# Attention and soft mixture of experts in one kernel: V's rows through two buffers up to pair 9, and another order of the last two pairs

## The chip, the cores and the metric

One core of a Trainium2 chip runs the whole kernel as one program. The metric is the device time of one execution in microseconds, and three executions give a median. Its engines are TensorE (PE, with its weight loads as PEld), VectorE (DVE), ScalarE (ACT), GpSimd (POOL) and SyncE (SP), which only issues transfers here. Each engine runs its instructions in the order in which they were issued to it, and waits for others by semaphores.

## The reference

```python
def _attn_ref(q, k, v, n_global, n_local):      # q, k, v: (4, 8, 768, 64)
    scores = scale * np.matmul(q, k.transpose(0, 1, 3, 2))
    ...
    keep = is_global | is_local                 # 8 global keys, 96 local ones, causal
    ...
    scores = np.where(keep, scores + bias, -1e9)
    a = softmax(scores)
    return np.matmul(a, v)

def _moe_ref(x, phi, w1, w2):                   # x: (3072, 512), 32 slots, 8 experts
    logits = x @ phi
    d = softmax(logits, over tokens)
    slot_input = d.T @ x
    for e in range(8):
        slot_out[e] = np.maximum(slot_input[e] @ w1[e], 0) @ w2[e]
    c = softmax(logits, over slots)
    return c @ slot_out
```

The bias is a slope per head times the distance. The output of the attention, (4, 768, 8 x 64), is the x of the expert layer. Softmax stands for the reference's own lines, with its small term in the divisor.

## The kernel before

There are 16 pairs (u = 0 to 15): four batches of four pairs of heads. For each pair the attention runs these steps, with i the head of the pair, k a third of the scores and z a third of the probabilities:

- load_qk, load_v (L418, L422): the transfers of q and k, and of V's rows (448 KB), issued by SP.
- v_hi or v_hi_act (L521, L524): V scaled to float16, on POOL for odd pairs and on ScalarE for even ones, into one of two buffers. v_lo (L527): what float16 leaves over, on VectorE. It reads V's rows once more and is their last reader.
- scores (L533) on TensorE; biased (L547) on VectorE adds the bias table and takes the running maximum.
- max_t, max_r, max_b, max_c: the maximum over the pair, by TensorE, VectorE, TensorE and ScalarE in turn. exponential (L570): on ScalarE, per head, with that maximum.
- w_hi (L579, ScalarE) or w_hi_dve (L583, VectorE): the float16 high part of the probabilities of one head. w_lo (L587, POOL) or w_lo_dve (L591, VectorE): the low part of a third z of one head, 128 x 432 elements. Both engines run it at line 589. There is one buffer for high parts and one for low parts, so w_hi of the next pair's head waits until TensorE has read the old one.
- values (L594): on TensorE, 39 small matmuls per head, thirteen each of high by high, high by low and low by high.
- ev_sum, ev_rec, ev_mul: VectorE divides by the row sums and writes x. tr, tr_copy: transposed x by TensorE and ScalarE. logits, logits_half, logits_all: x @ phi, two pairs at a time. by_token, dispatch, dispatch_sum and others: the expert layer's dispatch, once in a batch.

All these steps stand in one hand-written list, ORDER (L56), which interleaves pairs: while values of pair u runs, scores of pair u + 2 or so are made. Each engine's own order follows from that list.

V's rows have one buffer, vraw (L358). A step ('load_v', u) issues the transfer once v_lo of pair u - 1 has read the buffer, and from pair 3 on it also issues a piece of the expert weights. The expert weights come in 32 pieces of 1 MB: steps 'piece' load twelve of them into buffers of their own (weights, 12 times 2048 columns of float32), and steps 'free' load others into the attention's buffers as they come free. All of them stand in SP's one queue with the loads of q, k and V, in ORDER's sequence.

After the list, last_dispatch finishes the dispatch, and then hidden, project and combine compute the experts and write the output from the same core.

Of the kernel before, what the change touches and what calls it, by code (L numbers as in the profile page):

```python
# [15 lines left out]
AF = mybir.ActivationFunctionType  # L16
ALU = mybir.AluOpType
# [4 lines left out]
B, H, S, D = 4, 8, 768, 64  # L22
# [4 lines left out]
NJ = 7  # L27
# [22 lines left out]
VC = NJ * 2 * D  # L50
TABW = 4 * QW
NW = 12
# [4 lines left out]
NP = H // 2  # L57
SW = 2 * KB
NEG = -1.0e30
V_SC = 2.0 ** 6  # L60
# [235 lines left out]
def tile_attention_moe(ctx: ExitStack, tc: tile.TileContext, qk, v, phi, w1, w2, nn, out):  # L296
    nc = tc.nc
# [29 lines left out]
    weights = [keep.tile([P, WP], F32, name=f"wp{i}") for i in range(NW)]  # L327
# [18 lines left out]
    xn01 = ap.tile([P, 2 * XH], F32, name="xn01")  # L346

    def own(name, w):

        return home_of[name] if name in home_of else ap.tile([P, w], F32, name=name)  # L350

    rq = [own(f"raw{i}", QKW) for i in range(2)]
    tbs = [own(f"tb{i}", TBW) for i in range(NTB)]
    whi = [own(f"hi{i}", HPW).bitcast(F16) for i in range(NHB)]
    wlo = [own(f"lo{i}", HPW).bitcast(F16) for i in range(NHB)]
    tabs = [own(f"tab{p}", TABW).bitcast(BF16).rearrange("p (i c) -> p i c", i=2) for p in range(NP)]
    by_head = "p (j i d) -> p j i d"
    vraw = own("vraw", VC).rearrange(by_head, j=NJ, i=2)  # L358
    v16 = [own(f"v{i}", VW) for i in range(2)]
    vhi = [w[:, 0:VHW].bitcast(F16).rearrange(by_head, j=NJ, i=2) for w in v16]  # L360
    vlo = [w[:, VHW:].bitcast(F16).rearrange(by_head, j=NJ, i=2) for w in v16]
    xn2 = own("xn2", XH)
    xnb = [a[0:KB].rearrange("p (t f) -> p t f", t=NJ) for a in (xn01[:, 0:XH], xn01[:, XH:], xn2)]
    xtb = [own(f"xt{i}", S) for i in range(3)]


    last = nu - 1
    spaces = []
    for name in leaves:
        t, a, b = used[name]  # L370
        spaces.append([(k, max(a, at) - at, min(b, at + WP) - at) for k, (bt, at) in enumerate(blocks) if bt is t and max(a, at) < min(b, at + WP)])
    held = []
    for name, i, *_ in ORDER:
        if name == "free":
# [25 lines left out]
    def load_w(pieces, c0=0, c1=WP):  # L400

        for k in pieces:
            m, e, half = piece(k)
            nc.sync.dma_start(out=places[k][:, c0:c1], in_=(w1, w2)[m][e][:, WP * half + c0:WP * half + c1])
# [17 lines left out]
    def load_v(u):  # L422
        nc.sync.dma_start(out=vraw, in_=v[u // NP, u % NP])
        if u > 2 and extras:
            k, c0, c1 = extras.pop(0)
            load_w([k], c0, c1)
# [51 lines left out]
    def late_constants():  # L478
        nc.gpsimd.tensor_tensor(out=i4, in0=ident[:, 0:32], in1=ident[:, 32:64], op=ALU.add)
        nc.gpsimd.tensor_tensor(out=i4, in0=i4, in1=ident[:, 64:96], op=ALU.add)  # L480
        nc.gpsimd.tensor_tensor(out=i4, in0=i4, in1=ident[:, 96:128], op=ALU.add)
        nc.gpsimd.memset(sl, 0.0)
# [38 lines left out]
    def v_hi(u):  # L521
        nc.gpsimd.tensor_scalar(out=vhi[u % 2][:, :, :, 0:D], in0=vraw, scalar1=V_SC, scalar2=0.0, op0=ALU.mult, op1=ALU.add)  # L522

    def v_hi_act(u):  # L524
        nc.scalar.activation(out=vhi[u % 2][:, :, :, 0:D], in_=vraw, func=AF.Copy, scale=V_SC)  # L525

    def v_lo(u):  # L527
        k = u % 2
        flat = "p j i d -> p (j i) d"
        nc.vector.scalar_tensor_tensor(out=vlo[k].rearrange(flat), in0=vraw.rearrange(flat), scalar=V_SC,  # L530
                                       in1=vhi[k].rearrange(flat)[:, :, 0:D], op0=ALU.mult, op1=ALU.subtract)
# [306 lines left out]
    def table_pair_act(p):  # L838
        table.pair(p, True)

    steps = dict(piece=piece_of, free=free, load_qk0=load_qk0, load_phis=load_phis, keys=keys, warm=warm,
                 table_even=table_even, table_odd=table_odd, table_pair=table_pair, table_pair_act=table_pair_act, load_qk=load_qk, load_v=load_v, v_hi=v_hi, v_hi_act=v_hi_act, v_lo=v_lo,
                 scores=scores, biased=biased, max_t=max_t, max_r=max_r, max_b=max_b, max_c=max_c, exponential=exponential, w_hi=w_hi, w_hi_dve=w_hi_dve, w_lo=w_lo, w_lo_dve=w_lo_dve,
                 values=values, ev_sum=ev_sum, ev_rec=ev_rec, ev_mul=ev_mul, tr=tr, tr_copy=tr_copy, tr_copy_dve=tr_copy_dve,
                 logits=logits, logits2=logits2, logits_half=logits_half, logits_all=logits_all, strip_max=strip_max, strip_exp=strip_exp,
                 strip_sum=strip_sum, by_token=by_token, by_token_copy=by_token_copy, lnat_copy=lnat_copy, dispatch=dispatch, dispatch_sum=dispatch_sum)
    late_constants()
    for name, u, *args in ORDER:
        steps[name](u, *args)
# [311 lines left out]
```

## Time and profile before

| what | value |
|---|---|
| median of three runs | 213.93 us (212.89, 213.93, 214.44) |
| the profiled execution | 211.82 us, of which 210.0 us are the span of its instructions |
| mean granted TensorE clock | 0.975 |
| TensorE, VectorE, ScalarE, POOL busy | 86%, 71%, 61%, 56% of the span |
| attention and dispatch | up to about 155 us |
| hidden, project and combine | about 155 to 198 us, the last transfers after that |
| DMA | 61.41 MB, 292 GB/s on average |

Times on the trace are counted from the start of the span. A row of the timeline reads: start, length (of all instructions that it merges), engine, line, operation, output<-input, shape, count, and in brackets how long the engine stood idle before it and what ended that. "wa" is the large block that holds most of the attention's buffers, "wp" an expert weight buffer, "x" and "m" are TensorE's output banks. The slices of the page are 5.25 us each.

### The profile page before, as it was taken

What the parts mean: (1) busy time and instruction counts of PE and PEld (TensorE: products, weight loads), DVE (VectorE), ACT (ScalarE), POOL (GpSimd) and SP (SyncE); (2) the same over time, 40 slices, a digit from 0 to 9 for tenths busy, and PEclk for the clock granted to TensorE, in tenths of its full rate; (3) what the DMA queues carried; (4) which work ended last, traced back from release to release, by engine and by line L of the source; (5) the groups of instructions that cost most, each with busy time, mean ns of one, the idle gap of its engine ahead of it and who ended that gap; (6) DMA issues with size and microseconds to landing.
All of it is one profiled execution on the core that took longest, in us unless ns stands there. A gap on an engine that the chain in (4) does not pass through costs nothing. (4 is left out here: it accounts for less than half of the span.)

```text
span 210.0 us, 6480 instructions
## 1 busy us (share of the span) xinstructions
PE 180.3 (86%) x2649; PEld 128.2 (61%) x2649; DVE 150.1 (71%) x376; ACT 127.7 (61%) x177; POOL 117.9 (56%) x142
## 2 busy tenths in 40 slices
PE   8779899879599989999999999787799999998300
PEld 2356688658387868878788886565343266655200
DVE  3989999499788878988888999394577450646600
ACT  2329899866589768979799979832304180442400
POOL 8345988598699896999989989860000000000000
PEclk9999999999999999999999999999999999999955
DMA  3759999989997976665376677999989999596890
GB/s 101 311 180 394 385 350 408 361 291 352 386 378 255 380 295 210 247 248 190 115 264 226 222 247 244 359 375 378 378 333 312 390 394 384 182 338 214 261 339 19
DMA packets 21096, 61.41 MB, mean 292 GB/s; under 512 B 2368, under 2 KB 9408, under 8 KB 19392
## 3 DMA queue, kind: packets, MB, share of 16 engines
q1 hardware_dynamic: 20912, 60.89, 80.1%
q8 instruction: 23, 0.38, 0.7%
q14 instruction: 17, 0.14, 0.2%
q10 hardware_dynamic: 144, 0.00, 0.0%
HBM read 54.59 MB, written 6.29 MB: 290 GB/s over the span
## 5 line engine op out<-in xcount | busy, mean ns | idle before, releaser
L589 POOL TENSOR_TENSOR wa<-wa 128x432 f16<-128x432 f32 x91 | 99.8, 1129 | 7.8 <-ACT wa L581 5.2
L541 PE MATMUL sc<-wa 64*128 64x216 f32 (+2 forms) x448 | 48.2, 342 | 2.7 <-DVE mx L551 1.9
L605 PE MATMUL x<-wa 128*128 128x65 f16 (+1 forms) x1248 | 44.6, 194 | 3.9 <-POOL wa L589 2.5
L605 PEld LDWEIGHTS <-wa 128*128 128x128 f16 x1248 | 40.3, 97 | 10.2 <-issue 5.1
L581 ACT CAST wa<-wa 128x1296 f16<-128x1296 f32 x31 | 39.3, 1266 | 8.8 <-PE x L605 7.9
L571 ACT ACTIVATE wa<-wa,nb 128x1296 f32<-128x1296 f32 x32 | 43.5, 1374 | 0.5
L541 PEld LDWEIGHTS sc<-wa 64*128 64x128 f32 x448 | 36.9, 186 | 9.5 <-issue 3.9
L551 DVE CUSTOM_DVE_ANT_1 wa<-sc,wa,mx 128x864 f32<-128x864 f32 x32 | 35.7, 1116 | 4.2 <-PE sc L541 2.1
L530 DVE SCALAR_TENSOR_TENSOR wa<-wa 128x896 f16<-128x896 f32 x16 | 23.2, 1449 | 4.8 <-POOL wa L522 4.5
L551 DVE CUSTOM_DVE_ANT_1 wa<-sc,wa 128x864 f32<-128x864 f32 x16 | 16.8, 1050 | 2.5 <-POOL wa L589 1.9
L639 ACT COPY wa<-m 128x480 f32<-128x480 f32 (+1 forms) x32 | 14.4, 473 | 6.1 <-PE m L634 6.1
L622 DVE CUSTOM_DVE_ANT_1 xn<-x,rc 120x448 f32<-120x448 f32 x24 | 14.8, 622 | 0.6
L522 POOL TENSOR_SCALAR wa<-wa 128x896 f16<-128x896 f32 x8 | 7.5, 941 | 11.7 <-DMA wa<-in_v_dram 10.4
L634 PE MATMUL m<-ident,xn 120*128 120x120 f32 x84 | 12.9, 277 | 1.1 <-DVE xmax L622 0.5
L525 ACT ACTIVATE wa<-wa 128x896 f16<-128x896 f32 x8 | 7.6, 952 | 9.0 <-DMA wa<-in_v_dram 8.2
L215 ACT COPY wa<-cp 128x512 f32<-128x512 f32 x12 | 6.6, 591 | 8.4 <-PE cp L212 8.2
L217 DVE COPY wa<-cp 128x512 f32<-128x512 f32 x12 | 7.7, 686 | 5.1 <-PE cp L212 3.8
L634 PEld LDWEIGHTS m<-ident,xn 120*128 120x128 f32 x84 | 8.5, 140 | 3.2 <-ACT wa L639 1.5
L122 PE MATMUL hp<-wp,sl 128*32 128x512 f32 x96 | 10.5, 593 | 0.0
L664 PE MATMUL m<-wa,phis 128*32 128x240 f32 (+1 forms) x128 | 9.5, 332 | 0.2 <-ACT wa L639 0.2
L212 PE MATMUL cp<-sots,ct 128*128 128x256 f32 x48 | 7.8, 300 | 1.0 <-DVE flag L885 1.0
L564 PEld LDWEIGHTS m<-mm,bsel 2*128 2x128 f32 x32 | 4.7, 183 | 6.0 <-DVE mm L561 3.5
(165 smaller groups left out, 205.3 us busy)
## 6 DMA issues: line engine op xcount, KB each, us to landing
wa<-in_qk_dram SPq DMA_DIRECT2D x15, 832.0 KB, 6.4
wp<-in_w_dram SPq DMA_DIRECT2D x12, 1024.0 KB, 8.1
wa<-in_v_dram SPq DMA_DIRECT2D x16, 448.0 KB, 3.7
out_dram<-wa SPq DMA_DIRECT2D x10, 512.0 KB, 4.0
wp<-in_w_dram SPq DMA_DIRECT2D x8, 512.0 KB, 7.7
wp<-in_w_dram SPq DMA_DIRECT2D x16, 256.0 KB, 6.0
wa<-in_w_dram SPq DMA_DIRECT2D x3, 432.0 KB, 5.8
wa<-in_w_dram SPq DMA_DIRECT2D x1, 1024.0 KB, 6.8
```

The lines of the kernel that those rows point to most:

```text
L122: nc.tensor.matmul(out=hp[n][32 * s:32 * s + 32, :], lhsT=slv(a, c, s), rhs=w1(e, c // 2)[:, (c % 2) * DF + 512 * n:(c % 2) * DF + 512 * n ...
L530: nc.vector.scalar_tensor_tensor(out=vlo[k].rearrange(flat), in0=vraw.rearrange(flat), scalar=V_SC, in1=vhi[k].rearrange(flat)[:, :, 0:D], ...
L541: nc.tensor.matmul(out=sc[:, i, at:at + n], lhsT=r_[r, KCOL[j]:KCOL[j] + KR], rhs=r_[r, KW + KB * j:KW + KB * j + n], start=True, stop=True)
L551: nc.vector.tensor_tensor_reduce(out=tbs[u % NTB].rearrange("p (i c) -> p i c", i=2)[:, :, BW * k:BW * k + BW], in0=scs.pop((u, k))[:, :, ...
L571: nc.scalar.activation(out=head(u, i), in_=head(u, i), func=AF.Exp, bias=nbs[u], scale=T_SC)
L581: nc.scalar.copy(out=h, in_=t)
L589: (engine or nc.gpsimd).tensor_tensor(out=w, in0=t, in1=h, op=ALU.subtract)
L605: nc.tensor.matmul(out=x[:, (D + 1) * t:(D + 1) * t + d], lhsT=w[:, c:c + P], rhs=vv[:, j, i, 0:d], start=(z == 0), stop=(z == len(ops) - ...
L622: nc.vector.tensor_tensor_reduce(out=xnb[(u // 2) % 3][:, :, c:c + D], in0=out_of(u, i)[:, :, 0:D], in1=rcs.pop((u, i)).unsqueeze(2).to_br ...
L634: nc.tensor.transpose(out=m[:, at:at + KB], in_=xnb[(u // 2) % 3][:, t, P * (p % 2):P * (p % 2) + P], identity=ident[0:KB, 0:KB])
L639: nc.scalar.copy(out=xtb[u % 3][:, a:a + n], in_=ms.pop((u, k))[:, 0:n])
L664: nc.tensor.matmul(out=ms[u][32 * s:32 * s + 32, 0:n], lhsT=phis[:, units[u - k][1], :], rhs=xtb[(u - k) % 3][:, SW * s:SW * s + n], start ...
```

## The change

V's rows get a second buffer, for odd pairs up to 9: the first 896 columns of the twelfth weight buffer, whose own piece (piece 11) is loaded later, after v_lo of pair 9. From pair 10 on there is one buffer again. Each slot of ORDER that loaded V of pair u now loads V of pair u + 1, and pairs 0 and 1 are loaded together at the start; from pair 11 on the slots are the old ones. In the last two pairs, seven low parts are on VectorE and five on POOL (before: four and eight), w_hi of pair 15's second head is on ScalarE, and the steps of pairs 14 and 15 and what stands between them are put in another sequence.

```diff
-vraw = own("vraw", VC).rearrange(by_head, j=NJ, i=2)
+vraw = [w.rearrange(by_head, j=NJ, i=2) for w in (own("vraw", VC), weights[NW - 1][:, 0:VC])]
+
+def raw_v(u):
+
+    return vraw[u % 2 if u < 10 else 0]
...
 def load_v(u):
-    nc.sync.dma_start(out=vraw, in_=v[u // NP, u % NP])
+    nc.sync.dma_start(out=raw_v(u), in_=v[u // NP, u % NP])
```

The scaling steps and v_lo read raw_v(u) in the same way. Of the list, the start and the slot of pair 10 (one step to a line):

```diff
 ('load_v', 0)
+('load_v', 1)
 ('scores', 0, 0)
...
 ('max_r', 0)
-('load_v', 1)
+('load_v', 2)
...
 ('ev_sum', 8, 0)
-('load_v', 10)
+('piece', 11)
```

Lines behind 358 stand four further down in the changed kernel (L422's load at L427 instead of L423, the low parts at L593 instead of L589, v_lo at L534 instead of L530).

SP's queue at the start. "in_v" is V, "in_qk" are q and k, "in_w" the expert weights; wp_95 is the twelfth weight buffer. Before:

```order
L420 DMA wa<-in_qk_dram 128x640
L423 DMA wa<-in_v_dram 128x896
L420 DMA wa<-in_qk_dram 128x1664
L420 DMA wa<-in_qk_dram 128x1664 [waits DMAHW2_49,DMAHW3_49,DMAHW1_49,PE_49]
L433 DMA phis<-in_phi_dram 128x128
L423 DMA wa<-in_v_dram 128x896 [waits DMAHW4_49,DMAHW0_49,DVE_49]
L404 DMA wp_85<-in_w_dram 128x2048
```

The same place after the change:

```order
L424 DMA wa<-in_qk_dram 128x640
L427 DMA wa<-in_v_dram 128x896
L427 DMA wp_95<-in_v_dram 128x896
L424 DMA wa<-in_qk_dram 128x1664
L424 DMA wa<-in_qk_dram 128x1664 [waits DMAHW2_49,DMAHW3_49,DMAHW1_49,PE_49]
L437 DMA phis<-in_phi_dram 128x128 [waits DMAHW0_49]
L427 DMA wa<-in_v_dram 128x896 [waits DMAHW4_49,DVE_49]
L408 DMA wp_85<-in_w_dram 128x2048
```

V of pair 1 moved ahead of q and k of pair 1 and waits for nothing; the slot that held it, which waits for VectorE's v_lo of pair 0, now loads V of pair 2.

VectorE from the row sums of pair 13's second head (first row) to those of pair 15's first head (last row). "128x2x216" at L589 and L593 is a low part, L530 and L534 are v_lo of pair 15, L585 is w_hi_dve, L561 and L565 are the maximum of pair 15, and L750 and L754 are dispatch_sum. Before:

```order
L612 TENSOR_TENSOR rsall<-x,eps 120x7
L616 RECIPROCAL rc<-rsall 120x7
L561 TENSOR_REDUCE mm_153<-m 1x1
...
L530 SCALAR_TENSOR_TENSOR wa<-wa 128x896
L612 TENSOR_TENSOR rsall<-x,eps 120x7
L616 RECIPROCAL rc<-rsall 120x7
L589 TENSOR_TENSOR wa<-wa 128x2x216
...
L750 SCALAR_TENSOR_TENSOR sacc<-sacc,al,m 128x512
L585 CAST wa<-wa 128x6x216
L589 TENSOR_TENSOR wa<-wa 128x2x216 x2
L612 TENSOR_TENSOR rsall<-x,eps 120x7
L589 TENSOR_TENSOR wa<-wa 128x2x216
```

After:

```order
L616 TENSOR_TENSOR rsall<-x,eps 120x7
L593 TENSOR_TENSOR wa<-wa 128x2x216
L565 TENSOR_REDUCE mm_153<-m 1x1
...
L593 TENSOR_TENSOR wa<-wa 128x2x216 x2
L534 SCALAR_TENSOR_TENSOR wa<-wa 128x896
L616 TENSOR_TENSOR rsall<-x,eps 120x7
...
L593 TENSOR_TENSOR wa<-wa 128x2x216 x2
L754 SCALAR_TENSOR_TENSOR sacc<-sacc,al,m 128x512
L616 TENSOR_TENSOR rsall<-x,eps 120x7
...
L593 TENSOR_TENSOR wa<-wa 128x2x216 x2
L616 TENSOR_TENSOR rsall<-x,eps 120x7
```

One low part of pair 14 now stands ahead of pair 15's maximum, two stand ahead of v_lo of pair 15, and pair 15's four stand two by two on both sides of dispatch_sum; the cast is gone.

POOL's last rows, from the scaling of V of pair 13 (first row) to the end of its attention work; "128x2x216" is a low part, "128x14x64" the scaling of V. Before:

```order
L522 TENSOR_SCALAR wa<-wa 128x14x64
L589 TENSOR_TENSOR wa<-wa 128x2x216 x11
L695 TENSOR_SCALAR al<-al 128x1
L589 TENSOR_TENSOR wa<-wa 128x2x216
L522 TENSOR_SCALAR wa<-wa 128x14x64
L711 TENSOR_SCALAR state<-state,al 128x1
L589 TENSOR_TENSOR wa<-wa 128x2x216 x6
```

After:

```order
L526 TENSOR_SCALAR wa<-wa 128x14x64
L593 TENSOR_TENSOR wa<-wa 128x2x216 x11
L699 TENSOR_SCALAR al<-al 128x1
L593 TENSOR_TENSOR wa<-wa 128x2x216
L526 TENSOR_SCALAR wa<-wa 128x14x64
L715 TENSOR_SCALAR state<-state,al 128x1
L593 TENSOR_TENSOR wa<-wa 128x2x216 x3
```

Behind the scaling of V of pair 15 (the second scaling), three low parts are left of six: one of pair 14 and two of pair 15.

On TensorE the values of pair 14's first head now come ahead of the dispatch and of the transposes of pair 13, and the values of pair 15's first head ahead of the transposes of pairs 13 (second part) and 12 (second part) and of their logits; the transposes of pair 14's first part come ahead of the last values.

More of the change, by code (lines that the diff above doesn't have):

```diff
@@ L521, in v_hi @@
     def v_hi(u):
-        nc.gpsimd.tensor_scalar(out=vhi[u % 2][:, :, :, 0:D], in0=vraw, scalar1=V_SC, scalar2=0.0, op0=ALU.mult, op1=ALU.add)
+        nc.gpsimd.tensor_scalar(out=vhi[u % 2][:, :, :, 0:D], in0=raw_v(u), scalar1=V_SC, scalar2=0.0, op0=ALU.mult, op1=ALU.add)
     def v_hi_act(u):
-        nc.scalar.activation(out=vhi[u % 2][:, :, :, 0:D], in_=vraw, func=AF.Copy, scale=V_SC)
+        nc.scalar.activation(out=vhi[u % 2][:, :, :, 0:D], in_=raw_v(u), func=AF.Copy, scale=V_SC)
     def v_lo(u):
@@ L529, in v_lo @@
         flat = "p j i d -> p (j i) d"
-        nc.vector.scalar_tensor_tensor(out=vlo[k].rearrange(flat), in0=vraw.rearrange(flat), scalar=V_SC,
+        nc.vector.scalar_tensor_tensor(out=vlo[k].rearrange(flat), in0=raw_v(u).rearrange(flat), scalar=V_SC,
                                        in1=vhi[k].rearrange(flat)[:, :, 0:D], op0=ALU.mult, op1=ALU.subtract)
```

2 lines of the change are left out of this document (1 added, 1 removed).

## Prediction

> **What bounds the kernel now.** I read the page's shares and its 40 slices first, then stretches of 8 us, then the waits of the engines, and last the timeline around each wait.
>
> ```profile
> PE 180.3 (86%) x2649; PEld 128.2 (61%) x2649; DVE 150.1 (71%) x376; ACT 127.7 (61%) x177; POOL 117.9 (56%) x142
> ...
> PE   8779899879599989999999999787799999998300
> ...
> POOL 8345988598699896999989989860000000000000
> ...
> DMA  3759999989997976665376677999989999596890
> ```
>
> POOL's share of 56% is an average over two stages: it works until slice 26 (about 141 us, the attention) and then never again, and while it works it is at 8 or 9 tenths. TensorE is at 9 in nearly every slice from 11 to 24. So three engines are nearly full in the attention, and the question is which of them stands still where.
>
> ```profile
> core 0: us, PE busy (x) PEld busy (x) DVE busy (x) ACT busy (x) POOL busy (x), PEclk, DMA share, GB/s
> 40.00:48.00 8.00, 6.36 (x120) 4.97 (x120) 7.39 (x13) 5.47 (x8) 8.00 (x8) 1.00 0.84 300
> 72.00:80.00 8.00, 7.42 (x134) 5.57 (x131) 5.37 (x14) 5.81 (x10) 8.00 (x9) 1.00 0.67 248
> 96.00:104.00 8.00, 8.00 (x137) 6.62 (x139) 6.94 (x19) 6.46 (x12) 8.00 (x9) 1.00 0.47 169
> ```
>
> The reader is to see that TensorE has no idle time at all around 100 us (8.00 of 8.00), at full clock, but loses 1.64 us (8.00 - 6.36) and 0.58 us in the two stretches before it. TensorE runs its steps in a fixed order, so idle time taken out of it ahead of 80 us moves all that follows, and work taken off another engine behind 80 us does not, until the last pairs.
>
> ```profile
> POOL wa L522 <- DMA wa<-in_v_dram: 10.4, 4, 5.3
> ...
> POOL wa L522 <- DVE rsall L612: 1.0, 1, 1.0
> ```
>
> L522 is the scaling of V on POOL, for odd pairs. It waits 10.4 us in four places for V's rows, 5.3 of it once at the start. The wait that is put down to VectorE's row sums (rsall) I count as V's load too: the scaling neither reads nor overwrites them.
>
> **The middle: V a pair ahead.** With one buffer, V of pair u can only be fetched when VectorE's v_lo (L530) of pair u-1 has read it, and the fetch stands in a queue behind others.
>
> ```profile
> 32.00 0.33 SPq L423 DMA_DIRECT2D wa<-in_v_dram  x1
> 48.01 0.33 SPq L423 DMA_DIRECT2D wa<-in_v_dram  x1
> ...
> 39.42 0.94 POOL L522 TENSOR_SCALAR wa<-wa 128x896 f16<-128x896 f32 x1 [2.23 <-DMA wa<-in_v_dram]
> 54.15 0.94 POOL L522 TENSOR_SCALAR wa<-wa 128x896 f16<-128x896 f32 x1 [2.40 <-DMA wa<-in_v_dram]
> ...
> 40.40 1.89 DVE L530 SCALAR_TENSOR_TENSOR wa<-wa 128x896 f16<-128x896 f32 x1 [2.70 <-POOL wa L522]
> 55.13 1.88 DVE L530 SCALAR_TENSOR_TENSOR wa<-wa 128x896 f16<-128x896 f32 x1 [1.40 <-POOL wa L522]
> ...
> 41.39 0.66 PE L605 MATMUL x<-wa 128*128 128x65 f16 x16 [0.56 <-POOL wa L589]
> 43.31 1.07 PE L541 MATMUL sc<-wa 64*128 64x216 f32 x12 [0.32 <-DVE mx L551]
> 45.15 1.29 PE L605 MATMUL x<-wa 128*128 128x65 f16 x37 [0.59 <-POOL wa L589]
> 57.26 0.38 PE L564 MATMUL m<-mm,bsel 2*128 2x1 f32 x2 [2.16 <-DVE mm L561]
> 74.50 1.30 PE L605 MATMUL x<-wa 128*128 128x65 f16 x37 [0.58 <-POOL wa L589]
> ```
>
> These rows are one chain, read downwards. V of pair 3 is issued at 32.00 and POOL starts on it at 39.42, 7.4 us later; V of pair 5 at 48.01 and 54.15, 6.1 us. POOL stands 2.23 and 2.40 us, VectorE's v_lo behind it 2.70 and 1.40 us, and TensorE then waits for POOL's low parts and for VectorE's maximum. In the changed kernel each slot of the queue still waits for the same v_lo, so nothing is issued sooner, but what lands is V of the pair after next. The slot at 32.00 brings pair 4 and the one before it pair 3, so V is there about a pair (some 7 us) before its use, against 6.1 to 7.4 us from issue to use in the worst of these rows.
>
> The sum for TensorE: around 40 to 48 us the whole 1.64 us, since all its gaps there stand behind the two V waits; at 57.26, VectorE's v_lo would have begun 1.40 us sooner, so of 2.16 us I take 1.40; at 74.50 the 0.58 us, for POOL is then ahead by more than that (the wait of 1.0 us of pair 7 goes as well). 1.64 + 1.40 + 0.58 = 3.6 us. Ends: 2.2 us if the gap at 57.26 stays (1.64 + 0.58), and 5.6 us if POOL's own waits for pairs 3, 5 and 7 all come back (2.23 + 2.40 + 1.0). I take 3.6, because TensorE's rows at 96 us leave it no slack to catch up with.
>
> Of the other moves here: piece 11's load goes behind v_lo of pair 9, since it overwrites the second buffer; it is read in the expert layer only, after 155 us, and costs nothing. The first small weight block goes one slot forward, the same bytes. From pair 11 on V has one buffer again, as before. The weight loads that follow a V load on the queue issue when they did.
>
> **The start.** Here a load and an overlap are added.
>
> ```profile
> 2.63 9.46 SPq L420 DMA_DIRECT2D wa<-in_qk_dram  x2
> ...
> 9.47 3.34 POOL L292 TENSOR_SCALAR wa<-wa 128x1728 bf16<-128x1728 bf16 x2 [3.17 <-DVE wa L286]
> 18.09 0.94 POOL L522 TENSOR_SCALAR wa<-wa 128x896 f16<-128x896 f32 x1 [5.28 <-DMA wa<-in_v_dram]
> ...
> 13.06 1.09 DVE L530 SCALAR_TENSOR_TENSOR wa<-wa 128x896 f16<-128x896 f32 x1
> 14.76 1.06 DVE L551 CUSTOM_DVE_ANT_1 wa<-sc,wa 128x864 f32<-128x864 f32 x1 [0.42 <-PE sc L541]
> ```
>
> V of pair 1 is now fetched ahead of the q and k of pair 1, which were issued at 2.63. VectorE gets the scores made from them at 14.76, 12 us later, where a load of 832 KB takes 6.4 us (the rows on DMA below). Its 448 KB take 1.5 us at the 300 GB/s of the stretch at 40 us, so some 4 us stay in hand and it costs nothing; if they did not, 1.5 us at most. POOL's scaling of pair 1 runs at 12.81 (9.47 + 3.34) instead of 18.09. The 5.28 us are no gain by themselves: the low parts behind it need ScalarE's first high part, and nothing on TensorE waits for POOL before 41 us. But it now lies beside VectorE's v_lo of pair 0 at 13.06. v_lo takes 1.09 us with POOL idle and 1.89 us beside POOL's work (the row at 40.40). So its price is between 0 and 0.69 us (13.75 - 13.06); by the nearer row, 0.69, less the 0.42 us that VectorE waits next anyway: +0.3 us.
>
> By the Trainium skill ("SBUF — State Buffer", section "Who interferes with whom"), a VectorE instruction with two SBUF inputs and a GpSimd instruction that reads SBUF exclude one another for the whole instruction. By that rule the 0.69 is paid in full before cover, without it 0; the pair of durations 1.09 and 1.89 agrees.
>
> **The last two pairs.** In pairs 14 and 15 POOL computes five low parts instead of eight and VectorE seven instead of four, and the high part of pair 15's second head goes from VectorE back to ScalarE.
>
> ```profile
> 130.30 0.28 DVE L561 TENSOR_REDUCE mm<-m 1x1 f32<-1x128 f32 x1 [0.25 <-PE m L558]
> 135.73 0.65 DVE L589 TENSOR_TENSOR wa<-wa 128x432 f16<-128x432 f32 x1 [0.94 <-ACT wa L581]
> 138.35 1.94 DVE L589 TENSOR_TENSOR wa<-wa 128x432 f16<-128x432 f32 x2
> 140.28 1.33 DVE L589 TENSOR_TENSOR wa<-wa 128x432 f16<-128x432 f32 x1
> ...
> L589 DVE TENSOR_TENSOR wa<-wa x5: 603/973/1417, 19.5 to 140.3; 128x432 f16<-128x432 f32 x5
> L589 POOL TENSOR_TENSOR wa<-wa x91: 999/1014/1975, 19.0 to 139.8; 128x432 f16<-128x432 f32 x91
> ...
> 133.06 1.29 PE L605 MATMUL x<-wa 128*128 128x65 f16 x37 [0.71 <-POOL wa L589]
> 140.34 1.29 PE L605 MATMUL x<-wa 128*128 128x65 f16 x37 [0.52 <-DVE wa L589]
> 142.45 1.35 PE L605 MATMUL x<-wa 128*128 128x65 f16 x39 [0.82 <-DVE xmax L622]
> ...
> 134.43 1.27 ACT L581 CAST wa<-wa 128x1296 f16<-128x1296 f32 x1 [0.98 <-PE x L605]
> ```
>
> A low part takes 1.01 us on POOL and 0.65 us on VectorE when the other is still; side by side, 1.33 us (1417 ns at most). The steps, on the clock of before:
> 1. Pair 14, head 0. VectorE's piece stands ahead of the maximum of pair 15. POOL's scaling of V (0.94 us from 129.8) holds it to 130.7, so it ends at 131.3, the maximum (0.28) at 131.6 instead of 130.6, and TensorE's values start at about 132.0 and end at 133.2, where they ended at 134.35 (133.06 + 1.29).
> 2. Pair 15, head 0. ScalarE's exponential is 1 us later with the maximum, so its high part, which began at 134.43, gains only some 0.3 us and ends at 135.4. Then POOL one piece (1.0) and VectorE two (0.55 each, after POOL's): 137.5. Before, the last of these three ended at 141.61 (140.28 + 1.33). TensorE's values end at about 138, not 141.63.
> 3. Pair 15, head 1. ScalarE's high part runs 137.1 to 138.4; VectorE's own was done at much the same time, just ahead of the pieces at 138.35. POOL one piece to 139.4, VectorE two to 140.5. TensorE, which meanwhile transposes pairs 12 to 14, starts the last values at about 140.65 instead of 142.45: 1.8 us sooner. What follows (sum, product, transposes, logits) hangs on them as before.
>
> Gain 1.8 us. Ends: 2.5 us if no piece is held up by the other engine; -1.4 us (a loss) if each of the four VectorE pieces of pair 15 takes 1.33 instead of 0.55 (4 x 0.8 = 3.2 more). I take 1.8: only one POOL piece is left in each group of three.
>
> **The sum.** -3.6 - 1.8 + 0.3 = -5.1 us. Against the profiled execution (span 210.0, 211.82 us in all) that is 206.7; the three runs have a median of 213.93, 2.1 above it, so the forecast for a median is 213.93 - 5.1 = **208.8 us**. Differences under 1% (2.1 us) are about what a measurement of this kernel cannot tell from none.
>
> **Does the expert layer follow?** DMA is at 9 or more in slices 25 to 33, so the weights could come too late for a TensorE that is 5 us early.
>
> ```profile
> 159.80 17.07 SPq L404 DMA_DIRECT2D wp<-in_w_dram  x18
> ...
> 188.70 2.80 PE L152 MATMUL a<-wp,wa 128*32 128x256 f32 x48
> wa<-in_qk_dram SPq DMA_DIRECT2D x15, 832.0 KB, 6.4
> ...
> wp<-in_w_dram SPq DMA_DIRECT2D x16, 256.0 KB, 6.0
> ```
>
> The last weights are issued by 176.9 (159.80 + 17.07) and land 6.0 us later, 182.9, for matmuls at 188.70. Even if the transfers moved not at all, 5.8 us are in hand, more than 5.1. I cost it at nothing; the cover is gone from a gain of 5.8 us on.
>
> **The rivals.**
> - *POOL is the bound, not TensorE.* Then each wait of POOL comes back: 5.6 + 1.8 - 0.3 = 7.1 us, of which the weights' 5.8 us in hand may clip some; 206.8. For it: POOL is at 8.00 of 8.00 in both stretches in which TensorE idles. Against: TensorE is at 8.00 around 100 us too. Chance 0.14. The Trainium skill ("Perfetto Trace Analysis", "Identifying the Most-Contended Engine") says that matmul busy time is no good measure of TensorE's headroom and that the busy share of weight loads is; by that rule, with PEld at 6.62 of 8.00 at its best, this rival holds. The rows of that stretch, where TensorE has no gap, do not bear it out so far.
> - *The middle gives nothing.* The loads land in time, but VectorE, at 7.39 of 8.00 at 40 to 48 us, fills the gaps that V leaves (its order is fixed too), or the queue delays the earlier fetches as much. Only the tail is left: 1.8 - 0.3 = 1.5 us, 212.4. Against: VectorE idles for 2.70 and 1.40 us at just these places. Chance 0.12.
> - *The tail gives back.* 3.6 - 1.4 - 0.3 = 1.9 us, 212.0. Chance 0.09.
> - *Slower: VectorE's low parts are held by POOL.* Five of the seven lie on the chain of the last pairs. At 0.55 us a piece the change saves 5.1 us; from 0.55 + 5.1/5 = 1.6 us a piece it saves nothing, and at 2.0 us, the longest that such a piece took on POOL behind v_lo (1975 ns), it costs 5 x 1.45 - 5.1 = 2.1 us: 216.1. Against: the slowest of the five on VectorE took 1417 ns. Chance 0.04.
>
> **Chances.** Forecast 0.61 (207.5 to 210.5 by itself); the others as given. The best ends (5.6 and 2.5 us, no price at the start) give 205.8; the poor ones of the forecast (2.2, 0, +0.69) 212.4. I set the range from 205.8 to 212.0, which leaves out the slower case and the worse half of the second rival. Faster by over 1% (under 211.8): 0.61 + 0.14 + 0.07 of the two rivals near 212 = 0.82; within 1%: 0.14; slower: 0.04.
>
> **What would show it.** Right: no wait of L522's counterpart for V before pair 11; V's first two loads back to back; TensorE's idle time in 40 to 64 us below 1.5 us; the last values 4.5 to 6 us sooner; POOL done with its low parts near 135 us. Wrong in the middle: TensorE's gaps there stay, with VectorE as releaser. Wrong in the tail: VectorE's pieces of pairs 14 and 15 near 1.3 us each, or TensorE waiting for them by over 1 us. The forecast falls if TensorE in fact runs its matmuls faster when fed sooner (too small a gain), or if a new wait stands ahead of the last values.

## The result, and the profile after

In the first comparison the changed kernel took 204.81 us (median of 4 runs, 203.61 to 207.4) against 213.41 us of the kernel before (4 runs, 210.96 to 214.44): a ratio of 0.9657 [0.9591, 0.9723]. The ratios here and below leave out the slow runs of both kernels, so they are not the quotients of the medians beside them (here 0.9597). Scaled to the 213.93 us that the prediction started from, that is 206.6 us [205.2, 208.0], where 208.8 was forecast in a range from 205.8 to 212.0. The direction and the range held; the gain was some 2 us larger than the forecast. Taken by itself the median of 204.81 lies 1.0 us below the range. Two more comparisons of the same pair gave 0.9701 [0.9649, 0.9753] and 0.9773 [0.9722, 0.9823], which scaled in the same way is 207.5 and 209.1 us. So by the three comparisons the gain lies between 4.9 and 7.3 us, where 5.1 was forecast.

The profile of the first comparison has 6.8 us of half clock near its start (more on that below), so "after" in what follows is the profile of the second, with 0.979 of full clock: span 203.1 us, 204.96 us in all. Its page:

```profile
PE 179.0 (88%) x2649; PEld 128.2 (63%) x2649; DVE 151.3 (75%) x378; ACT 129.1 (64%) x178; POOL 113.8 (56%) x139
...
PE   8868699999899999999999999997799999997400
...
POOL 7363879999989996998989989630000000000000
```

Before, TensorE had a 7 in the ninth slice (42.0 to 47.2 us) and a 5 in the eleventh (52.5 to 57.8 us). Now it is at 8 or 9 in every slice from the sixth to the twenty-seventh (25 to 137 us). The stretches of 8 us say the same in numbers (the columns are those of the prediction's table):

```profile
core 0: us, PE busy (x) PEld busy (x) DVE busy (x) ACT busy (x) POOL busy (x), PEclk, DMA share, GB/s
40.00:48.00 8.00, 7.94 (x149) 6.34 (x149) 7.53 (x18) 6.83 (x9) 8.00 (x8) 1.00 0.95 358
72.00:80.00 8.00, 8.00 (x157) 6.29 (x154) 6.88 (x19) 7.03 (x8) 6.03 (x7) 1.00 0.74 264
96.00:104.00 8.00, 7.96 (x138) 6.11 (x136) 7.04 (x20) 6.37 (x8) 7.20 (x9) 1.00 0.58 202
```

TensorE went from 6.36 to 7.94 and from 7.42 to 8.00. And POOL's waits, after:

```profile
POOL wa L593 <- ACT wa L585: 12.8, 12, 4.6
...
POOL wa L593 <- PE m L638: 2.6, 1, 2.6
POOL wa L526 <- PE sc L545: 0.8, 1, 0.8
```

No transfer of V stands among them any more (10.4 us in four places before). The one wait left at L526, the scaling of V, is in pair 11 at 96.9 us, POOL's first scaling with the single buffer again; as in the prediction I count it as V's load, since the scaling reads nothing of the scores that are named. POOL now waits for ScalarE's high parts (12.8 us in twelve places, 5.2 us in seven before).

Where the time came from is read best from VectorE's row sums (L612 before, L616 after), which follow TensorE's values of each head. First three rows of before, then the same three of after: pair 0's first head, pair 13's second, pair 15's second; and last TensorE's combine (L212), before and after.

```profile
24.35 0.14 DVE L612 TENSOR_TENSOR rsall<-x,eps 120x7 f32<-120x7 f32 x1
129.66 0.16 DVE L612 TENSOR_TENSOR rsall<-x,eps 120x7 f32<-120x7 f32 x1
143.84 0.17 DVE L612 TENSOR_TENSOR rsall<-x,eps 120x7 f32<-120x7 f32 x1 [0.46 <-PE x L605]
...
24.98 0.14 DVE L616 TENSOR_TENSOR rsall<-x,eps 120x7 f32<-120x7 f32 x1
126.02 0.16 DVE L616 TENSOR_TENSOR rsall<-x,eps 120x7 f32<-120x7 f32 x1
137.79 0.17 DVE L616 TENSOR_TENSOR rsall<-x,eps 120x7 f32<-120x7 f32 x1 [0.48 <-PE x L609]
...
192.72 0.95 PE L212 MATMUL cp<-sots,ct 128*128 128x256 f32 x6 [1.01 <-DVE flag L885]
186.67 1.07 PE L212 MATMUL cp<-sots,ct 128*128 128x256 f32 x7 [1.01 <-DVE flag L889]
```

| stretch | before, us | after, us | difference | forecast |
|---|---|---|---|---|
| start, to the first row sums | 24.35 | 24.98 | +0.63 | +0.3 |
| middle, to those of pair 13 | 105.31 | 101.04 | -4.27 | -3.6 |
| last two pairs, to the last row sums | 14.18 | 11.77 | -2.41 | -1.8 |
| expert layer, to the combine | 48.88 | 48.88 | 0.00 | 0 |
| from there to the end of the span | 17.3 | 16.4 | -0.9 | 0 |
| span | 210.0 | 203.1 | -6.9 | -5.1 |

The last line but one is no effect of the change that I can name: in the twelve profiles of the experiments that stretch takes 15.9 to 17.3 us, and both numbers lie within it. The other lines are what the experiments were about.

### The profile page after: what moved, and what is told of

Read it like the earlier page. It is cut to its first block, busy times and chain, and to the rows that moved or that the text cites. A ratio compares the mean times of both kernels' runs of the same rounds, so it can differ in the third digit from the quotient of the medians.

```text
span 205.5 us, 6482 instructions
## 1 busy us (share of the span) xinstructions
PE 181.8 (88%) x2649; PEld 130.4 (63%) x2649; DVE 151.2 (74%) x378; ACT 129.2 (63%) x178; POOL 113.5 (55%) x139
## 4 chain that ended last, share of the span: by engine, by line
## 5 line engine op out<-in xcount | busy, mean ns | idle before, releaser
L593 POOL TENSOR_TENSOR wa<-wa 128x432 f16<-128x432 f32 x88 | 96.0, 1118 | 19.1 <-ACT wa L585 18.9
L545 PE MATMUL sc<-wa 64*128 64x216 f32 (+2 forms) x448 | 50.3, 357 | 2.1 <-DVE mx L555 1.2
L585 ACT CAST wa<-wa 128x1296 f16<-128x1296 f32 x32 | 40.6, 1268 | 7.8 <-PE x L609 6.6
L545 PEld LDWEIGHTS sc<-wa 64*128 64x128 f32 x448 | 39.3, 198 | 8.8 <-issue 3.5
L609 PE MATMUL x<-wa 128*128 128x65 f16 (+1 forms) x1248 | 43.8, 193 | 0.5 <-issue 0.3
L534 DVE SCALAR_TENSOR_TENSOR wa<-wa 128x896 f16<-128x896 f32 x11 | 16.0, 1452 | 0.0
L562 PE MATMUL m<-ident,mx 128*1 128x128 f32 x32 | 6.3, 279 | 2.5 <-DVE mx L555 1.9
L152 PE MATMUL a<-wp,wa 128*32 128x256 f32 x128 | 8.3, 384 | 0.0
L212 PE MATMUL cp<-sots,ct 128*128 128x256 f32 x48 | 7.4, 297 | 1.0 <-DVE flag L889 1.0
```

Source lines behind the costliest of these rows:

```text
L545: nc.tensor.matmul(out=sc[:, i, at:at + n], lhsT=r_[r, KCOL[j]:KCOL[j] + KR], rhs=r_[r, KW + KB * j:KW + KB * j + n], start=True, stop=True)
L585: nc.scalar.copy(out=h, in_=t)
L593: (engine or nc.gpsimd).tensor_tensor(out=w, in0=t, in1=h, op=ALU.subtract)
L609: nc.tensor.matmul(out=x[:, (D + 1) * t:(D + 1) * t + d], lhsT=w[:, c:c + P], rhs=vv[:, j, i, 0:d], start=(z == 0), stop=(z == len(ops) - ...
```

## The experiments

The question was twofold: are the parts what the prediction said, and is TensorE the bound in the middle (theory A, the prediction's) or POOL (theory B, its first rival)?

**The changed kernel again**, nothing edited.

> The changed kernel itself, unchanged, for its profile at full clock and as the measure of the others. In the first profile of it TensorE's granted clock was 0.5 from 13.1 to 19.9 us, and the row sums of pair 0 came 2.0 us later than before the change. Theory A (TensorE is the bound in the middle, the gain is its own gaps): without that stretch the row sums of pair 0 come at 24.3 to 24.8 us as before the change, those of pair 13 some 3.5 us sooner than before the change, the last ones some 5.5 us sooner, and the time against the kernel before is 0.970 to 0.976. Theory B (POOL is the bound): pair 13 comes 5 us or more sooner, the last 7, and the ratio is 0.965 or less.

204.93 us (204.3 to 206.22, 6 runs), ratio 0.9701 [0.9649, 0.9753]. This is the "after" above. A's numbers held for pair 13 (3.64 us sooner), for the last row sums (6.05 us) and for the ratio, but pair 0's row sums came at 24.98, later than it had said; B's 5 and 7 us did not come.

**V's buffers alone.** The list of steps is the changed one up to the high parts of pair 14 and the old one from there (in short):

```diff
-ORDER = changed
+ORDER = changed[:k] + before[k:]      # k: behind ('w_hi', 14, 1)
```

> The two buffers for V and the loads a pair ahead, with the old order and engines of the last two pairs. Theory A: 3.6 us less in the middle and 0.3 more at the start, so 3.3 us of 213.4, ratio 0.985. Theory B: 5.6 - 0.3 = 5.3 us, ratio 0.975. If the middle gives nothing (VectorE fills the gaps): 1.00. In the trace A wants the values of pair 14 to begin 3 to 4 us sooner than before and the wait of TensorE for POOL at that place (0.71 us) unchanged.

207.8 us (207.35 to 209.76), ratio 0.9855 [0.9798, 0.9912]. As A wanted, TensorE's wait for POOL in the values of pair 14 is 0.71 us again, and they go on behind it 4.0 us sooner (at 129.02 instead of 133.06).

**The last two pairs alone.** The same cut the other way round, with V's single buffer and the old loads.

> The new order and engines of the last two pairs alone, with V's single buffer. Both A and B: 1.8 us less, ratio 0.992; the two parts add up to the whole if they do not need each other. If the tail gains only because POOL arrives there ahead of its work (a theory C, the parts need each other), 0 to 0.5 us, ratio 0.998 to 1.00.

208.62 us (207.59 to 211.78), ratio 0.9867 [0.9808, 0.9926]. The row sums of pair 13 and the last ones, first of V's buffers alone, then of the last two pairs alone (whose profile has 6.8 us of half clock near the start, ahead of these rows):

```profile
125.62 0.16 DVE L616 TENSOR_TENSOR rsall<-x,eps 120x7 f32<-120x7 f32 x1
139.80 0.17 DVE L616 TENSOR_TENSOR rsall<-x,eps 120x7 f32<-120x7 f32 x1 [0.45 <-PE x L609]
...
132.27 0.16 DVE L612 TENSOR_TENSOR rsall<-x,eps 120x7 f32<-120x7 f32 x1
144.17 0.17 DVE L612 TENSOR_TENSOR rsall<-x,eps 120x7 f32<-120x7 f32 x1 [0.61 <-PE x L605]
```

With V's buffers alone the last stretch takes 14.18 us, to the hundredth what it took before; with the new order alone 11.90, 2.28 less (1.8 was expected). So the two parts don't touch each other there, and they add up: 0.9855 x 0.9867 = 0.972, against 0.970 for both. The rivals "the middle gives nothing" and "the tail gives back" fall with these two.

**More work for POOL.** In pairs 8 to 13 one low part is computed twice.

```diff
+('w_lo', u, 1, 1)      # ahead of the one that is there, u = 8 to 13
```

> The changed kernel with one low part of each of the pairs 8 to 13 computed twice on POOL (the same numbers again): six more instructions of 1.01 us on POOL, 6.1 us. Theory A: POOL waits for ScalarE's high parts there, so most of it is hidden: 0 to 2 us more than the changed kernel, and TensorE stays without gaps. Theory B: all of it shows, 5 to 6 us more (ratio against the changed kernel 1.025 to 1.03).

209.07 us (208.65 to 210.88), ratio 0.991 [0.9872, 0.9948].

**More work for TensorE.** In the same pairs the first third of the scores is computed twice.

```diff
-        for j in BANK_J[k]:
+        for j in BANK_J[k] * (2 if k == 0 and 8 <= u < 14 else 1):
```

> The changed kernel with the first third of the scores of pairs 8 to 13 computed twice on TensorE (the same numbers again): six times 8 matmuls, 0.93 us each, 5.6 us. Theory A (TensorE is the bound past 80 us): all of it shows, 5 to 5.6 us more than the changed kernel, ratio to the kernel before 0.996. Theory B (POOL is): 0 to 2 us more, ratio 0.97 to 0.98. Theory D (after the run with more POOL work, which cost 4.4 of 6.1 us: both are bounds within half a microsecond a pair): 4 to 5.6 us.

208.96 us (208.44 to 209.19), ratio 0.9837 [0.978, 0.9895]. What was added is less than the 5.6 us I had put in, as the groups of TensorE's scores from 60 to 130 us show (of the changed kernel, then of this one):

```profile
L545 PE MATMUL sc<-wa 64*128 64x216 f32 x160 | 20.6, 371 | 0.0
L545 PE MATMUL sc<-wa 64*128 64x216 f32 x208 | 24.9, 365 | 0.0
```

48 matmuls more took 24.9 - 20.6 = 4.3 us.

**Less work for POOL.** The low part that was doubled above is left out, so this kernel uses an old low part of the probabilities for a third of one head in pairs 8 to 13.

> The changed kernel with one low part left out in each of the pairs 8 to 13 (TensorE multiplies what the pair before left in that part of the buffer): 6.1 us less work on POOL. Theory A and D: TensorE has no gap there to lose, so 0 to 0.5 us less than the changed kernel, ratio to the kernel before 0.968 to 0.970. Theory B: 3 to 6 us less, ratio 0.94 to 0.955.

205.76 us (204.24 to 206.09), ratio 0.9659 [0.9596, 0.9722]. The three together are read from the row sums of pair 5's first head and pair 13's second, between which all the edits lie (VectorE; after, more POOL, more TensorE, less POOL, one pair of rows each; the second row of "after" is 126.02 above, and the last profile has 6.8 us of half clock ahead of its rows):

```profile
60.27 0.17 DVE L616 TENSOR_TENSOR rsall<-x,eps 120x7 f32<-120x7 f32 x1 [0.50 <-PE x L609]
...
59.79 0.17 DVE L616 TENSOR_TENSOR rsall<-x,eps 120x7 f32<-120x7 f32 x1 [0.50 <-PE x L609]
129.96 0.17 DVE L616 TENSOR_TENSOR rsall<-x,eps 120x7 f32<-120x7 f32 x1 [0.35 <-PE x L609]
...
59.77 0.17 DVE L616 TENSOR_TENSOR rsall<-x,eps 120x7 f32<-120x7 f32 x1 [0.50 <-PE x L609]
129.68 0.16 DVE L616 TENSOR_TENSOR rsall<-x,eps 120x7 f32<-120x7 f32 x1
...
61.41 0.17 DVE L616 TENSOR_TENSOR rsall<-x,eps 120x7 f32<-120x7 f32 x1 [0.50 <-PE x L609]
126.95 0.16 DVE L616 TENSOR_TENSOR rsall<-x,eps 120x7 f32<-120x7 f32 x1
```

| edit in pairs 8 to 13 | added, us | pair 5 to 13, us | shows |
|---|---|---|---|
| none | | 65.75 | |
| POOL, six low parts more | +6.1 (6 x 1.01) | 70.17 | +4.42 |
| TensorE, 48 matmuls more | +4.3 | 69.91 | +4.16 |
| POOL, six low parts fewer | -6.1 | 65.54 | -0.21 |

Work added to TensorE shows almost whole (4.16 of 4.3). Work taken off POOL does not show: in eight other profiles in which these pairs are as in the changed kernel the stretch takes 65.54 to 65.79 us, and 65.54 lies within that. So from pair 5 on TensorE is the bound, as theory A has it. But POOL stands close behind: of 6.1 us added only 6.1 - 4.42 = 1.7 us vanish, 0.3 us a pair. A had expected 0 to 2 us to show here and B 5 to 6, so 4.42 is neither's number; theory D, put up after this run, is about it: two bounds within half a microsecond a pair. TensorE then waits for POOL's low parts:

```profile
PE x L609 <- POOL wa L593: 3.8, 4, 1.7
...
86.82 1.03 PE L609 MATMUL x<-wa 128*128 128x65 f16 x28 [0.36 <-POOL wa L593]
103.83 1.30 PE L609 MATMUL x<-wa 128*128 128x65 f16 x37 [1.72 <-POOL wa L593]
120.26 1.30 PE L609 MATMUL x<-wa 128*128 128x65 f16 x37 [1.45 <-POOL wa L593]
```

The whole-kernel times alone would have misled: more work on either engine costs about as much (209.07 and 208.96 us, on two chips), which looks like two bounds at once. Only the kernel with less work, and what was added in each, tell them apart.

**The start, V of pair 1 on ScalarE**, which sits idle there, so that POOL no longer works beside VectorE's v_lo of pair 0.

```diff
 ('table_pair_act', 1)
+('v_hi_act', 1)
...
-('v_hi', 1)
```

> The changed kernel with V of pair 1 scaled on ScalarE, which idles there, instead of POOL. If VectorE's first v_lo (1.70 us against 1.09) is late because POOL's scaling lies beside it, it takes 1.09 us again, the row sums of pair 0 come at 24.35 us instead of 24.98, and the whole is 0.3 to 0.6 us shorter than the changed kernel (ratio to the kernel before 0.967 to 0.969). If the second V load at the start is what delays pair 0, v_lo and the row sums stay as they are in the changed kernel.

207.51 us (204.45 to 210.36), ratio 0.9675 [0.9602, 0.9748]: a wide spread, with a stretch of half clock from 27.1 to 30.5 us in its profile, which hides what was asked. So the next one adds idle matmuls to keep TensorE at work at the start.

```diff
-('warm', 0, 6)
+('warm', 0, 10)
...
-('warm', 0, 2)
+('warm', 0, 6)
```

> As the run before, with 4 more idle matmuls in each of the two stretches at 9 and 12 us in which TensorE has nothing to do. In two of the profiles so far TensorE's clock was granted at 0.5 from 13.1 to 20.3 us, and the row sums of pair 0 came 1.4 to 2.2 us later. If those idle stretches bring it on, no execution shows it, the highest of the runs is within 1 us of the median, and the median is 0 to 0.4 us lower. If not, the spread stays as it is (2 us above the median).

204.79 us (204.14 to 205.62), ratio 0.9637 [0.9591, 0.9683], with no such stretch. Two edits were now mixed, so the next four, side by side on one chip, take them apart: the changed kernel, each edit by itself, and both.

> The changed kernel once more, beside the next three on one chip. Both theories below: about 205 us, ratio to before near 0.970 (0.965 to 0.975). By the theory that short stretches of half clock come from TensorE's idle time at 10 to 13 us, its runs should spread over 2 us or more (they did: 204.3 to 206.2 and 203.6 to 207.4).

206.36 us (204.58 to 207.73), ratio 0.9773 [0.9722, 0.9823].

> V of pair 1 scaled on ScalarE ahead of its first wait, not on POOL. Theory A (the price of the start is VectorE's v_lo of pair 0 beside POOL's scaling, some 0.6 us, and TensorE behind is full so that it comes back whole): v_lo of pair 0 at 1.09 us instead of 1.70, row sums of pair 0 at 24.35 instead of 24.97, and 0.4 to 0.6 us off the time of the changed kernel. Theory B (the gain is swallowed by the wait for q and k of pair 3 at 24.7 us, or by the end): within 0.2 us of the changed kernel.

205.01 us (203.92 to 207.39), ratio 0.972 [0.9668, 0.9772].

> Only the idle matmuls at the start are more, 6 to 10 and 2 to 6; V of pair 1 stays on POOL. If idle time of TensorE at 10 to 13 us brings on the stretches of half clock: no run above 206 us, a spread of 1.5 us or less, the median at that of the changed kernel or up to 0.3 us lower. If it has nothing to do with them: the same spread as the changed kernel. v_lo of pair 0 stays at 1.70 us and the row sums of pair 0 stay at 24.97.

204.35 us (203.46 to 204.96), ratio 0.9696 [0.9652, 0.974].

> Both edits. In the one look at it so far it took 204.79 us (204.14 to 205.62), against 204.93 (204.3 to 206.22) of the changed kernel in another comparison on another chip. Theory A: 0.4 to 0.6 us under the changed kernel on the same chip, ratio to before 0.962 to 0.968. Theory B: the same as the changed kernel within 0.2 us.

204.37 us (204.05 to 204.7), ratio 0.9694 [0.9654, 0.9734].

v_lo of pair 0 (L534) and what follows it on VectorE, first of the changed kernel, then with V of pair 1 on ScalarE:

```profile
13.06 1.70 DVE L534 SCALAR_TENSOR_TENSOR wa<-wa 128x896 f16<-128x896 f32 x1
14.68 0.27 DVE L565 TENSOR_REDUCE mm<-m 1x1 f32<-1x128 f32 x1
16.37 1.12 DVE L555 CUSTOM_DVE_ANT_1 wa<-sc,wa,mx 128x864 f32<-128x864 f32 x1 [0.44 <-PE sc L545]
...
13.07 1.09 DVE L534 SCALAR_TENSOR_TENSOR wa<-wa 128x896 f16<-128x896 f32 x1
14.08 0.27 DVE L565 TENSOR_REDUCE mm<-m 1x1 f32<-1x128 f32 x1
24.51 0.14 DVE L616 TENSOR_TENSOR rsall<-x,eps 120x7 f32<-120x7 f32 x1
```

POOL's scaling at 12.88 us is what holds v_lo: take it away and 1.70 is 1.09 again. 0.47 of the 0.63 us come back at the first row sums (24.98 to 24.51, where 24.35 was expected). In the time of the kernel this cannot be told. Without the idle matmuls it is 205.01 us against the changed kernel's 206.36, but three of six executions of the latter had a mean granted clock of 0.957 or less, and one of six of the former. With the idle matmuls in both, V of pair 1 on POOL or on ScalarE gives 204.35 and 204.37, though in their profiles the last row sums came at 137.22 and 136.67: theory B's difference. In these two profiles the half microsecond is lost behind the start of the combine, where 16.5 and 17.2 us are left of the span; that length varies by more than this from one profile to the next.

The idle matmuls were the edit that counted: 204.35 against 206.36 on the same chip, 2.0 us where 0 to 0.3 was expected, and a spread of 1.5 instead of 3.2 us. Both kernels that have them were faster than before and, by the medians, than the changed kernel; their intervals overlap its interval a little (0.9652 to 0.974 and 0.9722 to 0.9823). In the second comparison, in which no execution of the changed kernel had a mean clock below 0.964, it took 204.93 us without them. So by these numbers they save the stretches of half clock and little else.

## Why the prediction was right, and where its sizes were off

**The bound.** "TensorE's rows at 96 us leave it no slack to catch up with" is shown, by 4.16 us of 4.3. The rival "POOL is the bound" named 206.8 us, nearer to the 206.6 of the first comparison than the forecast, but for a wrong reason: POOL has 0.3 us a pair to spare. The rule from the Trainium skill ("Perfetto Trace Analysis", "Identifying the Most-Contended Engine") that was weighed there, to judge TensorE's headroom by the share of its peak that the matmuls use and by the busy share of its weight loads, would by the second of these have promised room: that share is 6.11 of 8.00 at 96 us. The measurement decides against it: 4.3 us more work found no room.

**The middle, -3.6 forecast, -4.27 measured.** The mechanism and the places were right: the scaling of V waits for no transfer before pair 11; TensorE's idle time from 40 to 64 us is 0.8 us (0.19 at 52.60 and 0.63 at 54.54), below the 1.5 set as the mark; at 57.26, 1.45 of the 2.16 us went (from pair 3's row sums to pair 4's 9.03 us before, 7.58 after), where I took 1.40. The term that was mis-sized is the first, "the whole 1.64 us" at 40 to 48 us. From the row sums of pair 2's first head to those of its second, the changed kernel takes 5.72 us (37.44 to 43.16) where before took 7.99 (36.46 to 44.45): 2.27 us. The trace shows why. Values of one head on TensorE, first before, with the wait within them, then after; the row behind each is the next step:

```profile
39.96 0.87 PE L605 MATMUL x<-wa 128*128 128x65 f16 x23
41.98 1.01 PE L664 MATMUL m<-wa,phis 128*32 128x240 f32 x16
...
40.94 1.36 PE L609 MATMUL x<-wa 128*128 128x65 f16 x39
42.23 1.01 PE L668 MATMUL m<-wa,phis 128*32 128x240 f32 x16
```

Before, the step took 41.98 - 39.96 = 2.02 us; after, 42.23 - 40.94 = 1.29. The wait cost 0.73 us, but the row at 41.39 shows 0.56 idle. Idle time is counted from the end of the last matmul, and each of these is shown with 193 ns although a new one starts every 30 ns or so (39 in 1.29 us). So a wait inside such a group costs some 0.16 us more than its idle time. The one at 45.15 is of the same kind; the one at 43.31, between two groups, cost 0.39 us (1.33 from the start of the logits before, 0.94 after) where its row shows 0.32. From the start of these values to the same step further on (49.86 before, 48.67 after) TensorE takes 9.90 and 7.73 us: 2.17 of the 2.27 us, where the rows from 40 to 48 us show 1.64 idle. The step with the wait at 74.50 took 2.05 us before (73.68 to 75.73) and 1.29 after: 0.76, against 0.58 + 0.16 = 0.74. Some 0.4 us went again between pairs 0 and 1: TensorE waits 1.13 us at 24.69 for the q and k of pair 3, which were issued at 17.16 us (before 16.99) and landed at 24.55 (before 23.57). Before, this wait was 0.51 us; in the other profiles with two V buffers and full clock it was 0.4 to 1.0, so it is not the change that sets it alone. In those of them that leave pairs 8 to 13 as they are, the middle takes 100.4 to 100.7 us and not 101.04, so this "after" shows the gain of the middle rather too small.

**The last two pairs, -1.8 forecast, -2.41 measured.** Here step 1 of the working went the other way. VectorE's first piece (L593) of pair 14 and the maximum (L565), then POOL's scaling of V (L526), then TensorE's first values of pair 14 and the last ones of pair 15, all after:

```profile
126.10 0.60 DVE L593 TENSOR_TENSOR wa<-wa 128x432 f16<-128x432 f32 x1
126.67 0.28 DVE L565 TENSOR_REDUCE mm<-m 1x1 f32<-1x128 f32 x1
...
126.16 1.33 POOL L526 TENSOR_SCALAR wa<-wa 128x896 f16<-128x896 f32 x1
134.24 1.01 POOL L593 TENSOR_TENSOR wa<-wa 128x432 f16<-128x432 f32 x1 [2.60 <-PE m L638]
...
127.45 1.35 PE L609 MATMUL x<-wa 128*128 128x65 f16 x39
136.40 1.35 PE L609 MATMUL x<-wa 128*128 128x65 f16 x39
```

I had POOL hold VectorE; VectorE's piece started 0.06 us ahead and it was POOL's scaling that took 1.33 instead of 0.94 us. So the maximum came at 126.67, on the clock of before (3.64 later) 130.3 and not 131.3, and the values of pair 14 at 131.1 instead of 132.0. Two of VectorE's seven pieces did run into POOL (1.43 us at most), the others took 0.60 to 0.7, and the last values started 6.05 us sooner (142.45 to 136.40; the mark was 4.5 to 6), at 140.0 on the clock of before, where 140.65 was forecast. POOL is done at 135.25, as the prediction's mark had it. That the engine which starts first goes on and the other is held is what the Trainium skill says ("SBUF — State Buffer", "Who interferes with whom"); the traces agree at both places, 1.70 for v_lo behind POOL's earlier start and 1.33 for POOL behind VectorE's. Where the two starts lie closer, the rows do not tell the order: before, POOL's low part at 131.02 took 1.98 us, and v_lo of pair 15, which is shown to start at 131.05, its usual 1.07.

**The start, +0.3 forecast, +0.63 measured.** v_lo of pair 0 grew by 0.61 us (1.70 - 1.09), near the 0.69 of the sum. The cover, "less the 0.42 us that VectorE waits next anyway", was smaller than I took it: behind v_lo stands the maximum of pair 0 (L565), TensorE waits 0.41 us for it at 15.01 before it makes the scores that come next, and VectorE then waits 0.44 us for them, only one step later, at 16.37. There VectorE is 0.41 us late (15.96 before), and 0.36 us where v_lo of pair 1 starts, about the 0.3 of the forecast. The other 0.27 us are in no term of the sum: v_lo of pair 1 grew too. It and the low part that POOL is at when it starts, first before, then after:

```profile
22.68 1.54 DVE L530 SCALAR_TENSOR_TENSOR wa<-wa 128x896 f16<-128x896 f32 x1
22.27 1.01 POOL L589 TENSOR_TENSOR wa<-wa 128x432 f16<-128x432 f32 x1
...
23.04 1.81 DVE L534 SCALAR_TENSOR_TENSOR wa<-wp,wa 128x896 f16<-128x896 f32 x1
22.89 1.01 POOL L593 TENSOR_TENSOR wa<-wa 128x432 f16<-128x432 f32 x1
```

Before, POOL's instruction had 0.60 us left at the start of v_lo (22.27 + 1.01 - 22.68), after 0.86, and v_lo took 0.45 and 0.72 us more than 1.09. At pair 0 the scaling had 0.76 us left (12.88 + 0.94 - 13.06), and v_lo took 0.61 more. So what v_lo loses is what POOL has left, less some 0.15 us. The second buffer is not the cause: in the profile of the first comparison, where POOL is idle from 24.79 to 26.11 us, the same v_lo starts at 25.17 and takes 1.09.

**The expert layer** followed exactly, as forecast: 48.88 us from the last row sums to the combine before and after. The weights came sooner too: the last landed at 177.8 us instead of 182.5, for matmuls at 182.65 instead of 188.70, so 4.9 us of cover are still there.

## What to carry to other kernels

Price a wait of a pipelined TensorE by the distance between two starts with and without it, not by the idle time of its row: here a wait inside a group of small matmuls cost 0.16 us more than it showed. To find which of two nearly full engines is the bound, give each more work and then take some away: here added work cost on both, and work taken off POOL, which is not the bound, gained nothing (less work for TensorE was not tried). And before an idle time behind an instruction is counted as cover, look whether what ends it hangs on that same instruction. When a load or a step moves, the engines meet at other places too: the second v_lo lost 0.27 us although nothing of it had been moved.

## What the runs showed of the hardware that was not expected

In some executions of these kernels TensorE's granted clock falls to half for 3.4 or 6.8 us early on, between 13 and 31 us. The rows of granted clock (in tenths, 40 slices) of the changed kernel beside the one with more idle matmuls, on one chip; behind them the engines' busy time from 10 to 13 us in the two (TensorE's is the first after the length):

```profile
PEclk9975999999999999999999999999799999999965
PEclk9999999999999999999999999999999999999955
...
10.00:13.00 3.00, 1.60 (x14) 1.04 (x14) 2.70 (x5) 1.07 (x1) 2.84 (x3) 1.00 0.20 42
10.00:13.00 3.00, 2.56 (x19) 1.37 (x18) 2.70 (x5) 1.06 (x1) 2.84 (x3) 1.00 0.20 40
```

The stretch lasts 6.8 us, from 13.4 to 20.2 us, and the first row sums come at 26.57 instead of 24.98. (The 7 further on is a second one, 3.4 us from 146.5 us.) It follows a stretch in which TensorE stands still for 1.4 of 3.0 us, in two waits of 1.30 and 1.04 us that begin at 9.4 and 12.3 us. These waits don't bring it on each time: the profiles of the kernel before (1.42 and 1.05 us) and of the second comparison (1.20 and 1.05) have them too, and no such stretch. With the idle matmuls (0.44 us of 3.0) none of three profiles showed one; of eleven without them five did. The mean clock of the executions says the same: with them 18 executions had 0.970 to 0.979, without them 8 of 28 executions of kernels with V's buffers and both parts of the change had 0.960 or less, and 7 of 40 of the kernel before, so the change alone is not what brings them. (Where the clock was lost is known for the profiled executions only.) Why only some executions fall is not settled. The Trainium skill ("TensorE: Matmul & The Clock Gate", "HAM oscillation — how this bites in real kernels") puts the rule as no idle gaps of more than about 3.4 us; here the stretch came behind two shorter ones in a row.
